# The first k by another queue in an attention and MLP kernel: fp32 load ahead of f, a split cast, the clamp on GpSimd

## The chip, the core and the metric

One core of one Trainium2 chip runs the kernel. The metric is the device time of one execution in microseconds; three timed runs gave 321.07, 321.27 and 321.29 us, median 321.27.

## What is computed

Eight batches of eight heads of attention with a forget gate (576 tokens, 64 columns a head), and behind it an MLP with GELU on the 4608 x 512 result:

```python
scores = scale * np.matmul(q, k.transpose(0, 1, 3, 2))
log_f = np.log(np.clip(f, 0.0001, 1.0))
cum = np.cumsum(log_f, axis=-1)
decay = cum[:, :, :, None] - cum[:, :, None, :]
scores = np.where(causal, -1000000000.0, scores + decay)
attn = softmax(scores)
x = np.matmul(attn, v)                 # heads side by side: 4608 x 512
out = gelu_tanh(x @ w_in) @ w_out      # 512 -> 2048 -> 512
```

q, k, v are fp32 (8, 8, 576, 64), f is fp32 (8, 8, 576), the weights are fp32, and the output is fp32 (4608, 512).

## The kernel before, in words

**Units.** Four heads are a quad, i = 0 to 15, two quads a batch. The MLP works on chunks c of 512 of the 4608 rows. Each batch's attention fills its part of `xT`, and the MLP takes its chunks from there. Matmuls are in bf16, the sums in PSUM in fp32.

**Order.** Everything is in an order written out by hand: `setup()` (line 703) issues the first instructions, and then `run` (line 844) reads tables of words, FRONT (line 71) for the first two quads, the first chunk and the way into the steady state, then SECOND, STEADY, FLUSH and LAST. Each word calls one entry of `ops` (line 786), which issues that step's instructions on whichever engines they run on. Each engine works through its own instructions in this order and waits on semaphores where it needs another's result. So the place of a word sets the place of its instructions in the queue of every engine it uses, the DMA queues of SyncE (SP) and GpSimd (POOL) among them.

**The words that matter here.**

- `B.n.cols` and `BK.i.n` (lines 255 and 261): n dummy matmuls into `idle_ps`, of 128, 256 or 512 columns; BK reads `kT`, so it waits for that transpose.
- `LP.t`: tile t (128 tokens) of v of batch 0 into `v_nat`; `LC` and `LV` are loads of v of later batches. `WI.c`, `WO.c`: pieces of the weights. `LK.i`, `LQ.i`: k and q of quad i. LP, LC, WI, WO, LK and LQ are on GpSimd's queue, and k, q and the weights are cast from fp32 to bf16 by the DMA.
- `TK.i`, `TQ.i` (lines 223 and 226): VectorE transposes `k_c` into `kT` and `q_c` into `qT`, in 32 x 32 blocks of 4-byte words.
- `SC` (line 727): the running sum of log f, a scan on VectorE. `CT` (line 745): TensorE transposes the sums into `cum_ps`. `CE.n` (line 751): ScalarE's exp of them, `wT`, for the first two quads (0) and the others (1). `w.0` and `W.0`: their bf16 copy `w_bf` on ScalarE or VectorE.
- `S.i.r` and `H.i.r.g` (line 267): scores of quad i, round r, for all heads or two of them (`ps_s`), with their exp on ScalarE into `pt`. `M` and `m`: the causal mask, on GpSimd or VectorE. For the first two quads the work is in four rounds of columns.
- `D.i.part` (line 364): the denominators, a product with `w_bf`, then transpose (`den`), reciprocal and transpose back on VectorE. `vw.i.part` (line 229): v times `wT` on VectorE. `V.i.x.part` (line 382): the product with `vw` and its scaling into `xT` on VectorE.
- `j`, `J`, `I`, `i`: the MLP's first product in parts, `F.c.n` and `f.c.n` its second, n steps; `f` splits each step's 128 columns of weights into four matmuls of 32.

**The start.** `setup()` issues f on SyncE's queue, then k of quad 0, q of quad 0, k and q of quad 1 on GpSimd's (`load_one`, line 207). VectorE fills constants, then clamps f (line 724), ScalarE takes its logarithm (line 725), and the first words go on from there: VectorE's order at the start is clamp, SC, TK.0, TQ.0, TK.1, TQ.1. TensorE's is 14 dummies, CT, dummies around TK.0 and TQ.0, and then S.0.0.

Of the kernel before, what the change touches and what calls it, by code (L numbers as in the profile page):

```python
# [16 lines left out]
def kernel(  # L17
# [69 lines left out]

    SECOND = """
        Y F.-1.99 T.0.1 T.0.2 LB.2.0 T.0.3 T.0.4 LB.2.1 I.0.0 LB.2.2 E.0.2.2 I.0.1 LB.2.3 TK.3 LK.5 LB.2.4 E.0.2.2 TQ.3 LQ.5 TQ.4 I.0.2 E.0.2.2 I.0.3
        E.0.2.1 TK.4 G.0 VW.3 I.0.6 I.0.7 G.1.1.2 X F.0.13 S.3.0 M.3.0 f.0.9 UW.0.1 D.2 f.0.9 S.3.1 M.3.1 V.2.0 f.0.12 S.3.2 M.3.2 CL.3 V.2.1 VW.4  # L90
        f.0.14 S.4.0 UW.0.2 M.4.0 D.3 f.0.10 V.3.0 UW.0.4 CL.4 UW.0.3 S.4.1 f.0.13 M.4.1 V.3.1 S.4.2 F.0.9 M.4.2 F.0.2 F.0.1
    """

    STEADY = """
        LK.4 LQ.4 Q.0.2 Y LB.2.0 T.0.1 T.0.2 LB.2.1 F.-1.2 Q.0.2 i.0.2.4 T.0.4 LB.2.2 i.0.2.4 T.0.3 Q.0.2 TQ.3 LQ.5 Q.0.2 F.-1.6 i.0.3.4 Q.0.2 Q.0.2
        LB.2.3 TK.3 LB.2.4 LK.5 i.0.3.4 Q.0.2 TK.4 TQ.4 F.-1.99 I.0.6 i.0.7 G.0 S.3.0 X G.1.1.2 f.0.16 M.3.0 D.2 VW.3 f.0.12 S.3.1 M.3.1 V.2.0 f.0.13
        S.3.2 M.3.2 CL.3 V.2.1 VW.4 f.0.15 S.4.0 D.3 f.0.10 V.3.0 M.4.0 CL.4 S.4.1 f.0.14 M.4.1 V.3.1 S.4.2 F.0.12 M.4.2
    """

    FLUSH = """  # L100
# [21 lines left out]
    def many(n, shape, dtype, name):  # L122
        return [singles.tile(shape, dtype, name=f"{name}{i}") for i in range(n)]
# [11 lines left out]
    vw = many(2, [128, NT + 1, 4, D], BF16, "vw")  # L135
# [4 lines left out]
    gT = singles.tile([128, N_FT, CH], BF16, name="gT")  # L140
# [7 lines left out]
    f_sb = f_all[0:BH, :]  # L148
# [58 lines left out]
    def load_one(src, dst, i):  # L207
        b, h0 = i // QPB, 4 * (i % QPB)
        return nc.gpsimd.dma_start(  # L209
            out=dst[i % 2].rearrange("p a d -> p (a d)"),  # L210
            in_=src[b, h0:h0 + 4].rearrange("h (p a) d -> (h p) (a d)", p=32))

    def transpose_words(src, dst):

        n = src.shape[1]
        return nc.vector.transpose(  # L216
            out=dst.rearrange("p s c -> p (s c)").bitcast(FP32)
                .rearrange("p (t a) -> p a t", a=n),
            in_=src.rearrange("p a d -> p (a d)").bitcast(FP32)
                .rearrange("p (a d) -> p a d", d=D // 2),  # L220
        )
# [15 lines left out]
    def copy_low(i, copy):  # L237
        return copy(vw[i % 2][64:128, LOW], vw[i % 2][0:64, 0])
# [462 lines left out]


    def setup():
        nc.sync.dma_start(out=f_sb, in_=f.rearrange("b h s -> (b h) s"))
        nc.scalar.preload_act_table_set("natural_log_exp_and_others")
        load_one(k, k_c, 0)
        load_one(q, q_c, 0)
        make_identity(nc, ident_f32)
        load_one(k, k_c, 1)
        load_one(q, q_c, 1)  # L710

        nc.vector.memset(idle, 0.0)
        nc.vector.memset(ones_f32, 1.0)
        nc.vector.memset(shift, -64.0)
        nc.vector.memset(wT[64:128, :, HIGH, :], 0.0)
        for t_ in kT:
            nc.vector.memset(t_[:, 0:64], 0.0)
            nc.vector.memset(t_[:, 64 + S:], 0.0)
        zeros()
        logs()  # L720
        idle_ps.append(psO.tile([128, 1024], FP32, name="idle_ps", tag="po"))

    def logs():
        nc.vector.tensor_scalar(f_sb, f_sb, 1e-4, 1.0, op0=ALU.max, op1=ALU.min)
        nc.scalar.activation(f_sb, f_sb, AF.Ln)

    def running_sums():
# [55 lines left out]
    def load_values(b, half):  # L783
# [112 lines left out]
```

## Time and profile before

The profiled execution's own numbers:

| | |
|---|---|
| time of the profiled execution | 321.58 us |
| span, first to last instruction | 319.9 us |
| granted TensorE clock, mean | 1.000 |
| PE, DVE, ACT, POOL busy | 314.1, 243.3, 213.0, 108.2 us |
| bytes moved by DMA | 33.41 MB in 47,491 packets |
| GpSimd's DMA queue (software) | 15.99 MB, 28.3% of 16 engines' span |
| SyncE's DMA queue (hardware) | 16.60 MB, 19.4% of 16 engines' span |

PE is TensorE's matmuls, DVE is VectorE, ACT ScalarE, POOL GpSimd, SP SyncE. In a row of the timeline stand the start and the duration in us from the span's start, engine, line, operation, output and inputs, shapes, and in brackets the idle time ahead of it with what ended it. A chain row has start, duration, engine, output and line, with the number of instructions merged. A row of transfers has the KB of one and the time from its issue to its landing.

### The profile page before, as it was taken

What the parts mean: (1) busy time and instruction counts of PE and PEld (TensorE: products, weight loads), DVE (VectorE), ACT (ScalarE), POOL (GpSimd) and SP (SyncE); (2) the same over time, 40 slices, a digit from 0 to 9 for tenths busy, and PEclk for the clock granted to TensorE, in tenths of its full rate; (3) what the DMA queues carried; (4) which work ended last, traced back from release to release, by engine and by line L of the source; (5) the groups of instructions that cost most, each with busy time, mean ns of one, the idle gap of its engine ahead of it and who ended that gap; (6) DMA issues with size and microseconds to landing.
All of it is one profiled execution on the core that took longest, in us unless ns stands there. A gap on an engine that the chain in (4) does not pass through costs nothing.

```text
span 319.9 us, 11741 instructions
## 1 busy us (share of the span) xinstructions
PE 314.1 (98%) x5292; PEld 220.7 (69%) x5311; DVE 243.3 (76%) x368; ACT 213.0 (67%) x248; POOL 108.2 (34%) x146
## 2 busy tenths in 40 slices
PE   8999999999999999999999999999999999999996
PEld 3467834445776567776778877767776786688785
DVE  7675638698978879879877998599886866597674
ACT  3676777866766776878667867787596744836610
POOL 8789625600340416400851065305610150000000
PEclk9999999999999999999999999999999999999999
DMA  7999998951273911594129411971002111010213
GB/s 125 229 199 196 207 234 202 220 150 37 54 130 103 200 22 37 115 209 77 37 75 223 104 39 30 209 160 38 5 33 68 35 33 38 24 43 2 98 35 99
DMA packets 47491, 33.41 MB, mean 104 GB/s; under 512 B 29777, under 2 KB 42193, under 8 KB 47441
## 3 DMA queue, kind: packets, MB, share of 16 engines
q0 software_dynamic: 9632, 15.99, 28.3%
q1 hardware_dynamic: 37664, 16.60, 19.4%
q8 instruction: 41, 0.67, 0.9%
q10 hardware_dynamic: 144, 0.07, 0.1%
q14 instruction: 10, 0.07, 0.1%
HBM read 36.85 MB, written 9.44 MB: 145 GB/s over the span
## 4 chain that ended last, share of the span: by engine, by line
PE 98%; DVE 1%; issue 1%
PE ps_w L619 31%; PE ps_h L403 19%; PE ps_s L285 10%; PE ps_q L539 10%; PE po L355 9%; PE ps_h L439 5%; PE pso L692 4%; PE ps_u L487 4%; PE idle_ps L258 3%; PE po_m L341 2%; PE ps_p L619 1%; PE ps_o L355 0%; PE idle_ps L264 0%; DVE xT L387 0%; PE cum_ps L749 0%
## 5 line engine op out<-in xcount | busy, mean ns | idle before, releaser
L293 ACT ACTIVATE pt<-ps_s 128x1024 bf16<-128x1024 f32 (+2 forms) x100 | 94.0, 991 | 37.5 <-PE ps_s L285 35.9
L299 POOL TENSOR_SCALAR_AFFINE_SELECT pt<-pt 128x512 bf16<-128x512 bf16 (+3 forms) x70 | 43.3, 629 | 108.3 <-ACT pt L293 85.6
L403 PE MATMUL ps_h<-xT,w_in_sb 128*128 128x512 bf16 (+1 forms) x307 | 65.5, 357 | 0.8 <-issue 0.2
L403 PEld LDWEIGHTS <-w_in_sb 128*128 128x128 bf16 x320 | 31.1, 98 | 26.5 <-issue 0.6
L411 ACT ACTIVATE gT<-ps_h 128x1024 bf16<-128x1024 f32 x34 | 34.6, 1018 | 20.3 <-PE ps_h L403 20.1
L619 PEld LDWEIGHTS <-gT 128*32 128x32 bf16 (+1 forms) x1177 | 43.9, 97 | 5.7 <-issue 2.2
L619 PE MATMUL ps_w<-w_out_sb,gT 128*32 128x256 bf16 (+1 forms) x996 | 42.7, 273 | 0.0
L619 PEld LDWEIGHTS <-gsum 128*32 128x32 bf16 (+1 forms) x909 | 35.1, 97 | 3.9 <-issue 1.7
L285 PE MATMUL ps_s<-qT,kT 32*128 32x64 bf16 (+5 forms) x896 | 35.2, 261 | 0.0
L555 DVE TENSOR_TENSOR usnap<-ps_q,usnap 128x1024 f32<-128x1024 f32 x15 | 17.9, 1221 | 17.3 <-PE ps_q L539 12.7
L619 PE MATMUL ps_w<-usum,gsum 128*32 128x256 bf16 (+1 forms) x752 | 29.8, 273 | 0.0
L233 POOL TENSOR_TENSOR vw<-v_nat,wT 128x1280 bf16<-128x1280 f32 (+1 forms) x12 | 27.4, 2279 | 2.7 <-DMA v_nat<-in_v_dram 2.4
L285 PEld LDWEIGHTS <-kT 32*128 32x128 bf16 x896 | 16.2, 92 | 16.8 <-issue 10.2
L636 DVE COPY snap<-ps_w 128x512 f32<-128x512 f32 x32 | 21.8, 682 | 6.5 <-PE ps_w L619 6.3
L550 ACT ACTIVATE gT<-usnap 128x1024 bf16<-128x1024 f32 x15 | 15.8, 1052 | 11.0 <-DVE usnap L555 10.7
L387 DVE TENSOR_TENSOR xT<-po,rb 128x576 bf16<-128x576 f32 x26 | 19.5, 751 | 4.6 <-PE po L355 4.4
L355 PE MATMUL po<-pt,vw 128*32 128x64 bf16 (+4 forms) x624 | 22.6, 278 | 0.0
L355 PEld LDWEIGHTS <-vw 128*32 128x32 bf16 x672 | 14.6, 97 | 9.6 <-issue 3.0
L216 DVE STREAM_TRANSPOSE kT<-k_c 128x576 f32<-128x576 f32 x16 | 19.4, 1244 | 2.1 <-DMA k_c<-in_k_dram 2.1
L216 DVE STREAM_TRANSPOSE qT<-q_c 128x576 f32<-128x576 f32 x16 | 19.8, 1245 | 0.3 <-DMA q_c<-in_q_dram 0.3
L209 POOL DMA_DIRECT2D k_c<-in_k_dram x16 | 9.1, 572 | 29.0 <-DVE kT L216 17.4
L539 PEld LDWEIGHTS <-w_in_sb 128*128 128x128 bf16 x160 | 15.6, 98 | 2.1
(135 smaller groups left out, 489.6 us busy)
## 6 DMA issues: line engine op xcount, KB each, us to landing
out_dram<-o_st SPq DMA_DIRECT2D x35, 256.0 KB, 2.2
k_c<-in_k_dram POOLq DMA_DIRECT2D x16, 288.0 KB, 5.5
q_c<-in_q_dram POOLq DMA_DIRECT2D x16, 288.0 KB, 6.6
v_nat<-in_v_dram SPq DMA_DIRECT2D x16, 256.0 KB, 5.3
v_nat<-in_v_dram SPq DMA_DIRECT2D x20, 128.0 KB, 5.3
v_nat<-in_v_dram POOLq DMA_DIRECT2D x8, 256.0 KB, 10.0
w_in_sb<-in_moe_w_in_dram POOLq DMA_DIRECT2D x8, 256.0 KB, 8.6
w_out_sb<-in_moe_w_out_dram POOLq DMA_DIRECT2D x4, 512.0 KB, 10.6
```

What stands on the lines that cost most here:

```text
L216: return nc.vector.transpose(out=dst.rearrange("p s c -> p (s c)").bitcast(FP32) .rearrange("p (t a) -> p a t", a=n), in_=src.rearrange("p ...
L233: return eng.tensor_mul(vw[i % 2][:, t0:t1], vb[:, t0:t1, h0:h0 + 4, :], wT[:, i, t0:t1, :].unsqueeze(3).to_broadcast([128, t1 - t0, 4, D]))
L285: nc.tensor.matmul(tiles[h // 2][:, h % 2, c0:c0 + nq], key_columns(i, key, h, c), qq[32 * h:32 * h + 32, q0:q0 + nq, c], start=(c == 0 an ...
L293: nc.scalar.activation(p[:, 2 * g:2 * g + 2, off:off + n], t[:, :, 0:n], AF.Exp, scale=scale)
L299: nc.gpsimd.affine_select(out=x, in_=x, compare_op=ALU.is_ge, fill=0.0, base=0, pattern=pattern, channel_multiplier=-1)
L355: nc.tensor.matmul(po[r0:r0 + w.shape[-1], 448 + q0:448 + q0 + nq], w, p[:, h, col:col + nq], start=(key in (0, "low")), stop=(key in ("lo ...
L387: nc.vector.tensor_mul(xT[:, 2 * u + x, r0 + s0:r0 + s1], po, rbs[i, part])
L403: nc.tensor.matmul(ph[:, j, n * cols:(n + 1) * cols], w_in_sb[:, dt, 128 * ft:128 * ft + 128], xT[:, dt, h0:h0 + cols], start=(dt == 0 and ...
L411: nc.scalar.activation(gelus(c, 2 * pr, 2), ph, AF.Gelu_apprx_tanh)
L539: nc.tensor.matmul(ps[:, k, HC * n:HC * n + HC], w[:, d, 128 * n:128 * n + 128], x[:, d, :], start=(first and n == 0 and d == 0), stop=(d ...
L619: nc.tensor.matmul(ps[c0:c0 + width, n, cols[0]:cols[1]], x[:, j, 128 * n + c0:128 * n + c0 + width], w[:, j, cols[0]:cols[1]], start=(fir ...
L636: copy(kept[name], ps)
```

## The change

k of quad 0 is loaded as fp32 by SyncE's queue, ahead of f, into memory that the GELU's output `gT` uses later; GpSimd's queue then begins with q of quad 0. The cast to bf16 is done by ScalarE (the right half of the columns) and by VectorE (the left half, as a product with ones), at the end of `setup()`. The clamp of f goes from VectorE to GpSimd, and clamp and logarithm become words of their own (`LG`, `LN`). FRONT is written anew in another order. The words of SECOND and STEADY are the same; only their lines are broken elsewhere. Lines behind the new code move down by up to 16.

```diff
+    first = gT.rearrange("p f n -> p (f n)").bitcast(FP32)[:, 0:S * D // 32]
+
+    def load_first():
+        nc.sync.dma_start(out=first, in_=k[0, 0:4].rearrange("h (p a) d -> (h p) (a d)", p=32))
+
+    def cast_first():
+        to, n = k_c[0].rearrange("p a d -> p (a d)"), 576
+        nc.scalar.copy(to[:, n:], first[:, n:])
+        nc.vector.tensor_mul(to[:, 0:n], first[:, 0:n], ones_f32[:, 0:1].to_broadcast([128, n]))
...
     def setup():
+        load_first()
         nc.sync.dma_start(out=f_sb, in_=f.rearrange("b h s -> (b h) s"))
         nc.scalar.preload_act_table_set("natural_log_exp_and_others")
-        load_one(k, k_c, 0)
         load_one(q, q_c, 0)
...
-        logs()
+        cast_first()
         idle_ps.append(psO.tile([128, 1024], FP32, name="idle_ps", tag="po"))
 
+    def clamp():
+        nc.gpsimd.tensor_scalar(f_sb, f_sb, 1e-4, 1.0, op0=ALU.max, op1=ALU.min)
+
     def logs():
-        nc.vector.tensor_scalar(f_sb, f_sb, 1e-4, 1.0, op0=ALU.max, op1=ALU.min)
         nc.scalar.activation(f_sb, f_sb, AF.Ln)
...
+        "LG": clamp,
+        "LN": logs,
```

The first words of FRONT, up to the first denominators, before:

```
B.1.128 B.1.512 B.1.256 SC B.8.512 B.1.256 B.1.512 B.1.128 LP.0 LP.1 CT B.2.512 WI.1 B.1.256 TK.0 B.1.128 B.1.128 BK.0.2 WI.0 LP.4
BK.0.1 B.1.512 CE.0 TQ.0 B.1.512 CE.1 LP.3 B.1.512 BK.0.1 S.0.0 B.1.128 B.1.128 LP.2 TK.1 M.0.0 w.0 WI.5 BK.0.1 B.3.512 WI.2 H.0.2.1
WI.3 B.1.128 TQ.1 BK.0.1 B.1.128 B.1.128 B.1.256 B.1.128 BK.1.1 B.1.512 H.0.1.0 WI.4 D.0.0 vw.0.0 vw.1.0 H.0.2.0 B.2.512 BK.1.1
```

and after:

```
LP.3 TK.0 B.1.128 B.1.512 LP.0 B.1.256 B.8.512 B.1.512 B.1.128 B.2.512 B.1.256 TQ.0 LG B.1.128 LP.1 LN SC TK.1 BK.0.2 S.0.0 B.1.512
BK.0.1 TQ.1 WI.1 B.1.512 BK.0.1 B.1.128 B.1.128 LP.2 H.0.2.0 BK.0.1 CT CE.0 W.0 WI.0 H.0.2.1 H.0.1.0 WI.3 WI.2 B.3.512 H.1.0.1 CE.1
B.1.128 B.1.128 B.1.128 B.1.128 vw.0.0 B.1.256 B.2.512 B.1.128 M.0.0 D.0.0 WI.4 H.1.0.0 LP.4 WI.5 M.1.0 LQ.2 H.0.1.1 M.0.1 WI.7
```

Further on, the same scores, masks, values and MLP parts stand in another order. In the output product of the first chunk (`pso`, line 692) 16 of its 64 steps are `F` and 48 `f`, where 31 and 33 were.

More of the change, by code (lines that the diff above doesn't have):

```diff
@@ new lines @@
+        V.0.0.0 V.0.1.0 BK.1.1 UT vw.1.0 B.1.128 B.1.512 H.0.3.0 B.1.512 H.0.3.1 D.1.0 H.1.2.0 M.0.3 V.1.0.0 WI.6 V.1.1.0 H.1.3.0 LK.2
+        j.0.0.4 H.1.1.0 H.1.3.1 j.0.0.4 j.0.0.8 RJ.0.0 M.1.3 H.1.2.1 VW.1.1 tr H.1.1.1 M.1.1 D.0.1 j.0.1.8 J.0.2 vw.0.1 GJ.0.0 j.0.1.8
+        V.0.0.1 LQ.3 V.0.1.1 PW.2.1 D.1.1 J.0.3 V.1.0.1 V.1.1.1 J.1.3 J.1.1 W.1 J.1.2 WO.0 F.0.1 WO.1 LK.3 GJ.0.1 WO.2 J.1.0 F.0.1 f.0.1
+        WO.3 TQ.2 LQ.4 TQ.3 U.0 f.0.1 LC.1.4 LC.1.1 f.0.1 LC.1.0 f.0.1 LC.1.3 f.0.1 LC.1.2 f.0.1 TK.2 LK.4 S.2.0 TK.3 f.0.10 S.2.2 M.2.2
@@ new lines @@
+        f.0.1 LK.5 f.0.8 S.2.1 PW.2.2 F.0.9 m.2.1 LV.2.1 S.3.0 m.2.0 vw.2 f.0.2 cl.2 LV.2.0 f.0.2 D.2 f.0.1 F.0.2 S.3.1 TK.4 f.0.4 LV.3.0
+        f.0.1 V.2.0 M.3.0 TQ.4 f.0.1 S.3.2 m.3.1 TK.5 VW.3 cl.3 LQ.5 F.0.1 LQ.6 F.0.1 M.3.2 f.0.3 V.2.1 UW.2.4 LK.6 f.0.1 S.4.1 f.0.6
+        H.4.2.0 D.3 VW.4 f.0.1 H.4.0.0 H.4.0.1 V.3.1 v.3.0 f.0.1 vw.5 H.4.2.1 F.0.1 I.1.0 U.1 U.2 I.1.4 TQ.5 I.1.5 LV.3.1 cl.4 U.3 I.1.1
+        I.1.3 F.1.2 TQ.6 G.0 I.1.6 I.1.2 I.1.7 TK.6 F.1.4 X G.1.1.2 F.1.7 S.5.0 LQ.7@m.3.1 F.1.2 M.4.2.3 LK.8 F.1.5 LK.7 F.1.2 m.4.2.2 F.1.5
@@ L98 @@
+        Q.0.2 Q.0.2 LB.2.3 TK.3 LB.2.4 LK.5 i.0.3.4 Q.0.2 TK.4 TQ.4 F.-1.99 I.0.6 i.0.7 G.0 S.3.0 X G.1.1.2 f.0.16 M.3.0 D.2 VW.3 f.0.12
+        S.3.1 M.3.1 V.2.0 f.0.13 S.3.2 M.3.2 CL.3 V.2.1 VW.4 f.0.15 S.4.0 D.3 f.0.10 V.3.0 M.4.0 CL.4 S.4.1 f.0.14 M.4.1 V.3.1 S.4.2 F.0.12
+        M.4.2
     """
```

28 lines of the change are left out of this document (8 added, 20 removed).

## The prediction

> **What bounds the kernel now.** I read the page first, then the chain of work that ended last.
>
> ```profile
> span 319.9 us, 11741 instructions
> ...
> PE 314.1 (98%) x5292; PEld 220.7 (69%) x5311; DVE 243.3 (76%) x368; ACT 213.0 (67%) x248; POOL 108.2 (34%) x146
> ...
> PE 98%; DVE 1%; issue 1%
> ```
>
> TensorE is busy, and on the chain, for 98% of the span. An edit elsewhere counts only if it lets TensorE start its real work earlier, or makes it wait. The profiled execution took 321.58 us, 1.7 us more than its span of 319.9; the three timed runs have a median of 321.27. I work out a difference and apply it to 321.27. The next view asks whether TensorE waits after the start: busy time by stretch.
>
> ```profile
> 16.00:30.00 14.00, 13.88 (x268) 9.41 (x264) 8.01 (x17) 11.52 (x16) 12.27 (x20) 1.00 1.17 196
> 30.00:45.00 15.00, 14.89 (x169) 10.28 (x167) 9.22 (x11) 9.92 (x10) 8.39 (x11) 1.00 1.18 221
> 45.00:60.00 15.00, 14.68 (x284) 6.56 (x277) 9.30 (x14) 11.42 (x15) 7.97 (x11) 1.00 0.99 210
> 60.00:75.00 15.00, 14.86 (x169) 7.13 (x164) 14.18 (x19) 10.79 (x13) 2.92 (x2) 1.00 0.69 157
> ```
>
> The first pair of numbers after the stretch is its length and TensorE's busy time. From 16 to 75 us TensorE idles 0.12 + 0.11 + 0.32 + 0.14 = 0.69 us in all. The last three columns are granted clock, DMA share and GB/s: the clock is full and the DMA engines are full until 60 us. So the reordered words have at most 0.7 us to win there; what can be won is in the first 16 us, where TensorE's busy time is partly dummies. The chain at the start, merged:
>
> ```profile
> 1.26 5.08 PE idle_ps L258 x14
> ...
> 6.38 0.69 PE cum_ps L749 x5
> 7.07 0.76 PE idle_ps L258 x5
> 7.83 0.65 PE idle_ps L264 x3
> 8.48 0.65 PE idle_ps L258 x3
> 9.12 0.22 PE idle_ps L264
> 9.34 0.45 PE ps_s L285 x16
> ...
> 10.88 0.39 PE ps_s L285 x4
> ...
> 12.35 0.56 PE ps_s L285 x8
> 12.91 0.28 PE po_m L341 x8
> ```
>
> `idle_ps` is a dummy. The first real product, S.0.0, starts at 9.34 (call it S), behind dummies; 0.69 us of real work (CT, `cum_ps`) stands ahead of it. What releases S is on the other engines:
>
> ```profile
> 0.81 0.58 SPq L704 DMA_DIRECT2D f_all<-in_f_dram  x1
> ...
> 1.30 0.72 POOL L209 DMA_DIRECT2D k_c<-in_k_dram  x1 [0.79 <-POOLq L880]
> ...
> 3.68 0.45 DVE L724 TENSOR_SCALAR f_all<-f_all 64x576 f32<-64x576 f32 x1 [0.19 <-DMA f_all<-in_f_dram]
> 4.17 0.68 ACT L725 ACTIVATE f_all<-f_all 64x576 f32<-64x576 f32 x1 [2.08 <-DVE f_all L724]
> 4.25 1.81 POOL L186 DMA_DIRECT2D v_nat<-in_v_dram  x2
> ...
> 4.88 1.35 DVE L728 TENSOR_TENSOR_SCAN f_all<-ones_f,f_all 64x576 f32<-64x576 f32 x1 [0.75 <-ACT f_all L725]
> 6.16 1.22 DVE L216 STREAM_TRANSPOSE kT<-k_c 128x576 f32<-128x576 f32 x1
> 7.24 1.22 DVE L216 STREAM_TRANSPOSE qT<-q_c 128x576 f32<-128x576 f32 x1
> ...
> 13.24 0.45 DVE L374 STREAM_TRANSPOSE den<-po_m 128x256 f32<-128x256 f32 x1 [0.85 <-PE po_m L341]
> ...
> 14.33 1.25 DVE L233 TENSOR_TENSOR vw<-v_nat,wT 128x512 bf16<-128x512 f32 x2
> ```
>
> VectorE runs clamp, scan, TK.0, TQ.0, and TQ.0 ends at 7.24 + 1.22 = 8.46. TensorE could begin then; its own dummies hold it 0.88 us longer. The transfers, with the time from issue to landing:
>
> ```profile
> f_all<-in_f_dram SPq DMA_DIRECT2D x1, 144.0 KB, 2.9
> ...
> k_c<-in_k_dram POOLq DMA_DIRECT2D x1, 288.0 KB, 4.1
> q_c<-in_q_dram POOLq DMA_DIRECT2D x1, 288.0 KB, 5.0
> ```
>
> f lands at 0.81 + 2.9 = 3.7. The first k is issued at 1.30 and lands at 5.4; VectorE, in its scan until 6.2, isn't waiting for it. q is issued next and lands at 7.0.
>
> **The sum.** With one TensorE order before and one after, the change in time is: later or earlier S, plus real work that moves behind S, plus dummies added behind S, plus new waits.
>
> *CT* moves behind S: +0.69 (row above). *Dummies*: the front words before hold 11,008 columns of dummies ahead of S.0.0 and 7,680 behind; the words after hold 8,064 and 7,936. Behind S that is 256 more, at 0.65/3 us per 512 columns (row at 8.48): +0.11. So the change pays only if S comes before 9.34 - 0.69 - 0.11 = 8.54.
>
> *S after.* VectorE now does the cast's half, TK.0, TQ.0. Let T be the landing of the fp32 k. The cast's VectorE half is 576 fp32 columns to bf16; the nearest row is vw at 14.33, two of 512 columns in 1.25, so 0.63 x 576/512 = 0.70. ScalarE's half is nearest to its own 576-column row, 0.68, and lies beside it. TK.0 and TQ.0 took 8.46 - 6.16 = 2.30. With 0.1 us for each of the waits on the DMA, on the casts and on TQ.0, S = T + 0.70 + 2.30 + 0.3 = T + 3.3. q, now first on GpSimd's queue, must be there by T + 2.0; it moves up one issue (0.72 us), to about 6.3, and is in time. TensorE's own floor: 7,040 columns of leading dummies at the slow starting rate (5.08 us for 5,888 columns) end at 1.26 + 6.07 = 7.33, and two more dummies after TK.0 make 7.76.
>
> *T* is the unknown: 576 KB by SyncE's queue, four times f. No row shows such a load, so from both sides. The view of the first 3.9 us of DMA, in slices of about 0.1 us:
>
> ```profile
> GB/s 0 1 0 0 0 0 0 0 0 0 0 0 0 0 0 0 0 0 0 0 0 0 165 142 165 71 331 355 284 213 71 24 24 95 142 118 189 142 118 260
> ```
>
> f's bytes begin at 2.2, are through by 3.0 at up to 355 GB/s, and the landing at 3.7 is 0.7 later. k alone at 355 GB/s: 590 KB take 1.66, so 2.2 + 1.66 + 0.7 = 4.5. That is the near end. The far end is sharing: GpSimd's queue delivers its first bytes at about 2.7, now q's, on the same 16 engines. A stretch of 0.5 us from 110 us, where both queues have work:
>
> ```profile
> q0 software_dynamic: 43, 0.09, 100.7%
> q1 hardware_dynamic: 36, 0.01, 10.4%
> ```
>
> q0 is GpSimd's queue, q1 SyncE's: 43 packets against 36, so they take turns by packet. The Trainium skill ("DMA: Bandwidth & Descriptors", Queues, rings and completion order) says that each DMA engine goes round the rows that have work, a packet at a time; the trace agrees (43 to 36), and it speaks against "ahead of f, ahead of everything". If q halves k's rate from 2.7 on, the 0.5 us before have moved 0.5/1.66 of k, the rest takes 2 x 1.16, and T = 2.7 + 2.32 + 0.7 = 5.7. I take T = 4.95, nearer to the end alone, because GpSimd's queue starts slowly: between 3.0 and 3.8 the slices show 24 to 189 GB/s with nothing else running. Then S = 8.25 and the gain is 8.54 - 8.25 = **0.3 us**. (The skill's same page, section Anatomy of one DMA, fits 2.0 us plus bytes over 436 GB/s; an estimate from it has k landing at 4.2 and the gain at TensorE's floor. Its 2.3 us for f is not what the row shows, 2.9.)
>
> *f behind k.* f's landing goes to about T + 0.8 = 5.8. The clamp on GpSimd: no such row; below is VectorE's 0.45, above GpSimd's two-input 768-column product:
>
> ```profile
> 24.60 1.52 POOL L233 TENSOR_TENSOR vw<-v_nat,wT 128x768 bf16<-128x768 f32 x1
> ```
>
> 1.52 x 576/768 = 1.14. I take 0.9, as it has one input. Then Ln, 0.68: done at 7.6. The scan now stands behind TQ.0, at 8.2, so this is covered by 0.6 us; and CT, the next to want it, stands behind S.0.0, 1.0 us of dummies and H.0.2.0, at about S + 2, while scan ends at 9.6. Cost nothing; if the clamp took 1.5 us longer, CT would be late by about 0.5. Taking the clamp from VectorE gains nothing either: it is ahead of the wait for k.
>
> *GpSimd's queue.* The clamp waits for f and holds back the issue of LP.1 and every load after it. It costs nothing while the engines have earlier loads to move: at 6.7 us k1, q1, LP.3, LP.0 are still ahead. W.0 on VectorE instead of ScalarE (0.2 us) is covered by the same dummies.
>
> *F to f.* 15 steps of the output product change from one 128-column matmul to four of 32. By form:
>
> ```profile
> L692 PE MATMUL pso<-w_out_sb,gT 128*32 128x512 bf16 x132 | 9.3, 381 | 0.0
> L692 PE MATMUL pso<-w_out_sb,gT 128*128 128x512 bf16 x27 | 7.2, 380 | 0.4 <-issue 0.3
> ```
>
> 9.3/33 = 0.28 against 7.2/27 = 0.27 a step: +0.2 at most, and as much may come back from fewer changes between the two shapes. I take 0. The remaining words are the same products in another order, with 0.69 us of idle time to win or to double.
>
> Sum: 8.25 - 9.34 + 0.69 + 0.11 = -0.29; 321.27 - 0.3 = **321.0 us**.
>
> **The rivals.**
>
> *k has the engines to itself.* T = 4.5, S = 7.8, at TensorE's floor: 7.8 - 8.54 = -0.74, and up to half of the 0.69 us idle with it: 320.2 to 320.6. For it: q's slow start. Against it: the packets in turn.
>
> *A new wait takes over: VectorE's vw.0.0.* It now stands ahead of the denominators' transpose (den), and needs LP.0 and LP.1. LP.1, the second of the two `v_nat` issues at 4.25, used to be issued at 5.2; now it stands behind the clamp, at 6.7 or later. The loads' rows:
>
> ```profile
> v_nat<-in_v_dram POOLq DMA_DIRECT2D x1, 256.0 KB, 7.8
> ```
>
> If that time from issue holds, LP.1 lands at 14.5, vw.0.0 ends at 15.2, and den, which TensorE would release at S + 5.7 (2.9 of products by the rows above, 6,272 columns of dummies 2.7, 0.1 of waits) + 0.3 = 14.2, starts 1.0 late; with f at 6.4, 1.6 late. That gives +0.7 to +1.3: 322.0 to 322.6. It decides if LP.1 lands after 13.5. Against it: LP.1 is the sixth load of the queue as before, when it landed at 5.2 + 7.8 = 13.0, so the time is set by what is ahead, not by its issue.
>
> *The change doesn't do what it says.* Sharing in full, T = 5.7, later than the software queue's 5.4: S = 9.0, +0.45: 321.4 to 321.8.
>
> **How the numbers follow.** Chances: the forecast 0.42 (its own range 320.7 to 321.4), k alone 0.28, the wait of vw.0.0 0.19, full sharing 0.11. About 0.2%, 0.64 us, is what a measurement of this kernel can tell from no change: faster lies below 320.63, slower above 321.91. The forecast gives 0.06 faster, 0.34 same, 0.02 slower; k alone 0.26 and 0.02; the wait is slower; full sharing 0.08 same, 0.03 slower. Together 0.32, 0.44, 0.24. The range, 319.9 to 322.3, leaves out the best of the reordering together with k alone, and the worst of the wait.
>
> **What would show it.** The landing of gT's load (4.5, 4.95 or 5.7); the first `ps_s` at T + 3.3; idle time of PE ahead of it where before there were dummies; `vw` ahead of `den` with a wait for a DMA or none; the scan with no wait ahead of it. I am wrong if S lies under 7.7, if TensorE's idle time from 16 to 75 us leaves 0.3 to 1.4, or if the scan waits for Ln.

## The result, and the profile after

The changed kernel takes 323.60 us (median of nine runs, 321.23 to 323.97) against 321.27 for the kernel before on the same chip: a ratio of 1.0055, 95% interval 1.0032 to 1.0078. It is slower, and the time lies above the forecast's range. (The ratio goes by the means, 322.94 and 321.17 us, and so lies below that of the medians; in e2 and e3 below it leaves out one disturbed run each, of 362.52 and 326.77 us.) The profiled execution took 323.97 us, 2.4 more than that of before: 1.8 in the span and 0.6 around it. Its page, with the lines shown of before:

```profile
span 321.7 us, 11794 instructions
PE 313.2 (97%) x5317; PEld 220.8 (69%) x5336; DVE 243.8 (76%) x367; ACT 214.0 (67%) x249; POOL 112.2 (35%) x147
PE 84%; DMA 9%; POOL 2%; ACT 2%; issue 1%; DVE 1%; DVEq 0%; POOLq 0%
```

The span is 1.8 us longer and TensorE is 0.9 us less busy. The chain, 98% TensorE before, now also runs over transfers and GpSimd. Busy time by stretch (columns as in the prediction):

```profile
16.00:30.00 14.00, 13.84 (x233) 9.12 (x233) 8.43 (x17) 12.61 (x19) 13.23 (x21) 1.00 1.11 178
30.00:45.00 15.00, 14.77 (x231) 10.84 (x226) 9.08 (x14) 8.82 (x10) 8.69 (x12) 1.00 1.12 179
45.00:60.00 15.00, 14.39 (x286) 6.62 (x283) 9.01 (x13) 10.84 (x13) 7.86 (x9) 1.00 1.02 225
60.00:75.00 15.00, 14.78 (x201) 7.20 (x199) 13.80 (x15) 11.60 (x13) 4.64 (x6) 1.00 0.91 197
```

From 16 to 75 us TensorE idles 0.16 + 0.23 + 0.61 + 0.22 = 1.22 us, against 0.69. This measure is rough: a second profile of the kernel before (e18 below) shows 0.14 us there, and it has records of 5311 matmuls where the first has 5292; a matmul without a record can count as idle time. The rest of the loss lies earlier, in the timeline of the start:

```profile
0.80 0.39 SPq L218 DMA_DIRECT2D gT<-in_k_dram  x1
...
1.30 0.74 POOL L211 DMA_DIRECT2D q_c<-in_q_dram  x1 [0.79 <-POOLq L896]
...
4.81 0.67 ACT L222 CAST k_c<-gT 128x576 bf16<-128x576 f32 x1 [2.73 <-DMA gT<-in_k_dram]
4.89 0.76 DVE L223 TENSOR_TENSOR k_c<-gT,ones_f 128x576 bf16<-128x576 f32 x1 [1.37 <-DMA gT<-in_k_dram]
...
5.76 1.26 DVE L228 STREAM_TRANSPOSE kT<-k_c 128x576 f32<-128x576 f32 x1
...
7.07 0.59 PE L276 MATMUL idle_ps<-kT,idle 128*128 128x512 bf16 x2 [0.57 <-DVE kT L228]
...
7.22 2.14 POOL L736 TENSOR_SCALAR f_all<-f_all 64x576 f32<-64x576 f32 x1 [1.84 <-DMA f_all<-in_f_dram]
...
8.07 1.26 DVE L228 STREAM_TRANSPOSE qT<-q_c 128x576 f32<-128x576 f32 x1 [1.06 <-DMA q_c<-in_q_dram]
9.39 0.83 PE L297 MATMUL ps_s<-qT,kT 32*128 32x256 bf16 x16 [1.73 <-DVE qT L228]
...
9.39 0.68 ACT L739 ACTIVATE f_all<-f_all 64x576 f32<-64x576 f32 x1 [3.91 <-POOL f_all L736]
9.42 0.94 POOL L188 DMA_DIRECT2D v_nat<-in_v_dram  x1
10.11 1.35 DVE L742 TENSOR_TENSOR_SCAN f_all<-ones_f,f_all 64x576 f32<-64x576 f32 x1 [0.78 <-ACT f_all L739]
...
14.27 1.00 DVE L245 TENSOR_TENSOR vw<-v_nat,wT 128x512 bf16<-128x512 f32 x1
...
16.58 0.45 DVE L386 STREAM_TRANSPOSE den<-po_m 128x256 f32<-128x256 f32 x1 [1.31 <-PE po_m L353]
```

The fp32 k lands at 4.8 and its cast and transpose are done at 7.0. Then VectorE waits 1.06 us for q, which the forecast had in place at 6.3 and which lands at 8.05. TensorE, out of dummies, waits 1.73 us and starts S.0.0 at 9.39, where the kernel before has it at 9.27. f lands at 7.14, the clamp on GpSimd takes 2.14 us, and the load behind it (LP.1) is issued at 9.42. The scan, at 10.11, waits for the logarithm.

The two waits of TensorE have a second price. The granted clock, third column from the right:

```profile
8.00:10.00 2.00, 0.61 (x16) 0.41 (x15) 1.26 (x1) 0.61 (x1) 1.94 (x2) 0.74 1.08 215
10.00:12.00 2.00, 2.00 (x14) 0.73 (x6) 1.89 (x2) 1.59 (x3) 2.00 (x4) 0.50 1.02 269
12.00:14.00 2.00, 2.00 (x25) 0.99 (x22) 1.72 (x3) 1.20 (x4) 2.00 (x3) 0.91 1.08 198
```

After 0.57 + 1.73 us of waiting the clock is halved for about 3.4 us ((0.26 + 0.50 + 0.09) x 2 us / 0.50). The Trainium skill ("TensorE: Matmul & The Clock Gate", Part 1: The HAM clock gate) says that the activity is judged in a free-running window of some 3.4 us. The traces agree in so far as the length of the waits alone doesn't decide: of the runs below, e7 waited 1.99 us in one piece and its clock fell, e9 waited 1.49 us and e4 even 2.76 + 0.49 us, and both kept theirs.

Where the 1.9 us come from can be added up, because TensorE's last matmul ends at S, the start of S.0.0, plus all that TensorE does and waits for behind it. (S is 9.27 before by the timeline; the prediction's 9.34 is the chain's figure for the same matmul.) Summed over TensorE's rows, in us, the second and third profiles being further executions of the same kernel:

| | S | waits behind S | dummies behind S | CT behind S | other products | end |
|---|---|---|---|---|---|---|
| before | 9.27 | 1.52 | 3.58 | 0 | 302.55 | 316.92 |
| before, second profile (e18) | 9.93 | 0.14 | 3.68 | 0 | 303.55 | 317.30 |
| after | 9.39 | 2.12 | 4.63 | 0.44 | 302.25 | 318.83 |
| after, second profile (e5) | 8.33 | 3.10 | 3.68 | 0.49 | 302.48 | 318.08 |
| after, third profile (e12) | 9.18 | 1.99 | 4.64 | 0.44 | 302.22 | 318.47 |

Between the first profiles, S gives +0.12 where the forecast had -1.09; waits +0.60; dummies +1.05, of which about 0.1 are the added columns and the rest is the halved clock; CT +0.44; other products -0.30. In the second profile of the changed kernel q came at 7.00, S at 8.33, close to the forecast's 8.25, and the clock stayed full. Even so the end is 1.2 us later than before: waits and other products together are 1.5 us longer. (They are better taken together, since a matmul without a record moves time from the one to the other, as the two profiles of before show.)

A mark that does not depend on missing records is the first product of the steady state, the first `ps_u`. From there to its last matmul TensorE takes 215.07 to 215.38 us in every profile of this document. From S to there it takes 92.6 and 92.3 us in the two profiles of before, and 94.4, 94.7 and 94.2 in the three after: 1.7 to 2.4 us more, where the forecast had 0.80. So two things have to be explained: q's arrival, and what takes longer between S and some 104 us.

### The profile page after: what moved, and what is told of

Read it like the earlier page. It is cut to its first block, busy times and chain, and to the rows that moved or that the text cites. A ratio compares the mean times of both kernels' runs of the same rounds, so it can differ in the third digit from the quotient of the medians.

```text
span 321.7 us, 11794 instructions
## 1 busy us (share of the span) xinstructions
PE 313.2 (97%) x5317; PEld 220.8 (69%) x5336; DVE 243.8 (76%) x367; ACT 214.0 (67%) x249; POOL 112.2 (35%) x147
## 4 chain that ended last, share of the span: by engine, by line
PE 84%; DMA 9%; POOL 2%; ACT 2%; issue 1%; DVE 1%; DVEq 0%; POOLq 0%
PE ps_w L631 31%; PE ps_h L415 19%; PE ps_q L551 10%; PE po L367 9%; PE ps_s L297 8%; PE ps_u L499 4%; DMA v_nat<-in_v_dram 4%; DMA k_c<-in_k_dram 3%; DMA q_c<-in_q_dram 2%; ACT pt L305 1%; PE idle_ps L270 1%; PE pso L704 1%; PE ps_p L631 1%; PE ps_o L367 0%; POOL w_out_sb L204 0%
## 5 line engine op out<-in xcount | busy, mean ns | idle before, releaser
L305 ACT ACTIVATE pt<-ps_s 128x1024 bf16<-128x1024 f32 (+2 forms) x100 | 94.1, 990 | 34.8 <-PE ps_s L297 34.7
L311 POOL TENSOR_SCALAR_AFFINE_SELECT pt<-pt 128x512 bf16<-128x512 bf16 (+3 forms) x71 | 45.8, 654 | 89.6 <-ACT pt L305 66.7
L297 PE MATMUL ps_s<-qT,kT 32*128 32x64 bf16 (+5 forms) x896 | 36.1, 263 | 1.9 <-DVE qT L228 1.7
L211 POOL DMA_DIRECT2D k_c<-in_k_dram x15 | 8.4, 558 | 32.9 <-DVE kT L228 31.0
```

Source lines behind the costliest of these rows:

```text
L297: nc.tensor.matmul(tiles[h // 2][:, h % 2, c0:c0 + nq], key_columns(i, key, h, c), qq[32 * h:32 * h + 32, q0:q0 + nq, c], start=(c == 0 an ...
L305: nc.scalar.activation(p[:, 2 * g:2 * g + 2, off:off + n], t[:, :, 0:n], AF.Exp, scale=scale)
L311: nc.gpsimd.affine_select(out=x, in_=x, compare_op=ALU.is_ge, fill=0.0, base=0, pattern=pattern, channel_multiplier=-1)
```

## The experiments

My theory after reading this profile: the load of k on SyncE's queue holds q back on GpSimd's, S is not earlier for it, and TensorE cools while it waits. The rivals: the clamp on GpSimd and the loads behind it set the end; or the new order of the words does. Each kernel is timed beside the kernel before on the same chip (medians 321.05 to 321.11).

**The words without the load (e1).** k goes back to GpSimd's queue, no cast; clamp on GpSimd and all new words stay.

```diff
     def setup():
-        load_first()
...
+        load_one(k, k_c, 0)
         load_one(q, q_c, 0)
...
-        cast_first()
```

> The changed kernel, but k of quad 0 comes by GpSimd's software queue in bf16 again, ahead of q, and there is no cast. The new words and the clamp on GpSimd stay. Theory A (the software queue's first load stands still while the hardware queue moves k and f, so q lands at 8.05, S.0.0 isn't earlier, and TensorE cools down while it waits): the software queue's first packet is back near 2.7 us, k lands near 5.4, q near 7.0, S.0.0 starts near 8.6, and the time is 321.0 to 322.2. Rival B (the new word order costs the time by itself): 322.8 or more. Rival C (the clamp on GpSimd holds the loads back): f lands at 3.7, so the clamp runs at about 6.1 to 8.2 and LP.1 is issued 1.2 us earlier than in the changed kernel; about 322.5.

Measured: 322.02 us, ratio 1.0029 (1.0018 to 1.0040). q lands at 7.42, S is at 8.76. The time is within what the theory allowed, but the words with the clamp are slower than before by themselves, and without the load q comes earlier, not later, than in the profile after.

**Dummies against the cold clock (e2).**

```diff
-... LN SC TK.1 BK.0.2 S.0.0 B.1.512
+... LN SC TK.1 BK.0.9 S.0.0 B.1.512
```

> The changed kernel with seven more dummies (BK.0.9 for BK.0.2) in TensorE's wait between TK.0 and S.0.0. Theory A: S.0.0 stays at 9.4, the granted clock stays 1.00 between 8 and 12 us, D.0.0 comes at about 15.0 instead of 16.2, and the time falls by 0.8 to 1.5 us, to 322 to 322.8. B and C: the half clock is covered by other waits, and the time stays within 0.4 us of the changed kernel's.

Measured: 324.69 us, ratio 1.0104 (1.0088 to 1.0120), above all three medians of the changed kernel (323.60, and 322.73 and 323.02 in e5 and e12 below). The clock was full throughout, but q landed at 8.60, so S was at 9.93, and TensorE then waited 0.25 us for the scan and 0.40 for the mask. Another 1.2 us went behind the last matmul (4.1 us to the end of the span against 2.9; the last `o_st` transfers to DRAM took 3.7 us from issue to landing against 2.2), which the edit doesn't touch. From S to the first `ps_u` this execution takes 94.1 us against 94.4 after. So a full clock won little here: where the cold clock stretched dummies in the profile after, TensorE waits here, for the scan and the mask. The last part of my theory isn't borne out, though q's late landing clouds the comparison.

**The clamp on VectorE (e3), and f ahead of k (e4).**

```diff
     def clamp():                                # e3
-        nc.gpsimd.tensor_scalar(f_sb, f_sb, 1e-4, 1.0, ...)
+        nc.vector.tensor_scalar(f_sb, f_sb, 1e-4, 1.0, ...)
     def setup():                                # e4
-        load_first()
         nc.sync.dma_start(out=f_sb, ...)
+        load_first()
```

> The changed kernel with the clamp on VectorE, at its new place behind TQ.0. Theory A: the clamp waits for TQ.0 at 9.3, scan is 0.4 us later, LP.1 and the loads behind it are issued 4 us earlier (5.4), but S.0.0 stays at 9.4 and the clock still falls: within 0.5 us of the changed kernel. Rival C: the loads' gain is the point, the weights land 1 us or more earlier, and the time falls by 0.8 us or more.

> The changed kernel with f ahead of k on SyncE's queue. Theory A: f lands at 3.7, k at about 5.2, the software queue's first packet is still held back until about 4.2, q lands at 8.0 to 8.2, S.0.0 at 9.4 to 9.6; time within 0.5 us of the changed kernel. Rival C: the clamp no longer waits for f, it ends near 7.6 instead of 9.4, LP.1 is issued 1.8 us earlier, and the time falls by 0.7 us or more. If the queues only took turns, q would land near 7.

Measured: e3 322.25 us, ratio 1.0036 (1.0025 to 1.0047); e4 323.76, ratio 1.0071 (1.0049 to 1.0094). With the clamp off GpSimd, LP.1 is issued at 5.3 instead of 9.4, and the time is 0.5 to 1.3 us below the changed kernel's three medians, or 0.5 to 0.8 by the ratios, which lies between the theory (within 0.5) and the rival (0.8 or more). LP.1 itself lands no sooner for it (13.78 against 14.18 after and 13.34 in e5). In e4 f lands at 3.84 but k only at 6.50, so S is at 9.86, and q lands at 7.01. That misses the theory, which wanted k at 5.2 and q at 8.0 to 8.2; it is what taking turns was said to give. GpSimd's first packet comes at 3.91, with less than half of k moved, and then both queues move packets, here from 4.4 to 5.2 us (q0 is GpSimd's queue, q1 SyncE's):

```profile
q0 software_dynamic: 36, 0.08, 55.4%
q1 hardware_dynamic: 37, 0.16, 51.0%
```

**The changed kernel again (e5, e12).** No edit; two more profiles on two more occasions.

> The changed kernel once more, as the measure for the runs beside it. Both theories: 322.9 to 324.0 us, first real product at 9.4, q landing at 8.0, granted clock near 0.5 from 10 to 12 us. If in a second profile the clock stays full there and the time does not fall, the cold clock is not part of the loss.

> The changed kernel a third time, as the measure for the runs beside it and for how far its own start varies: 322.5 to 323.7 us, runs 1.5 us or more apart; f landing between 5.5 and 7.6 and q between 7.0 and 8.6, S.0.0 at q's landing plus 1.3.

Measured: 322.73 us, ratio 1.0061 (1.0037 to 1.0084), and 323.02, ratio 1.0051 (1.0032 to 1.0069). q landed at 7.00 and at 7.84, f at 6.19 and 7.15; e5 missed the expected 8.0 for q and 9.4 for S. The granted clock of each timed run is on record too. Of the 22 runs of the changed kernel in its three timings, six show 0.989 to 0.995, with a mean of 323.9 us, and sixteen show 0.999 or 1.000, with a mean of 322.6; no run of e1, and none of the kernel before in all these timings, shows less than 0.998. The fallen clock and the late q come together in the profiles (8.05 and 7.84 against 7.00), so this doesn't separate them. Together they add 0.4 us to the mean of 322.9, and without such runs the changed kernel is still 1.4 us slower than before.

In e5 nothing is cold and S is early, so its timeline shows what else waits:

```profile
8.33 0.52 PE L297 MATMUL ps_s<-qT,kT 32*128 32x256 bf16 x16 [0.54 <-DVE qT L228]
...
11.52 1.23 DVE L228 STREAM_TRANSPOSE qT<-q_c 128x576 f32<-128x576 f32 x1
...
12.60 0.16 DVE L793 CAST w_bf<-wT 128x40 bf16<-128x40 f32 x1
...
12.80 0.51 PE L297 MATMUL ps_s<-qT,kT 32*128 32x256 bf16 x8 [0.26 <-DVE w_bf L793]
13.13 1.69 POOL L311 TENSOR_SCALAR_AFFINE_SELECT pt<-pt 128x512 bf16<-128x512 bf16 x2
...
13.44 0.90 DVE L245 TENSOR_TENSOR vw<-v_nat,wT 128x512 bf16<-128x512 f32 x1 [0.68 <-DMA v_nat<-in_v_dram]
...
14.87 0.23 PE L353 MATMUL po_m<-pt,w_bf 128*1 128x128 bf16 x4 [0.41 <-POOL pt L311]
```

The first of S.0.0's exps have been ready since 9.8, but GpSimd masks them only at 13.13: behind the clamp (to 8.42) stand 4.7 us of issuing held-back loads. TensorE waits 0.41 us for the mask, and 0.26 ahead of H.1.0.1. The profile puts these 0.26 us down to W.0 (`w_bf`), but H.1.0.1 reads `qT`, not `w_bf`, and TQ.1 ends at 12.75, just as long before it. TQ.1 stands on VectorE behind the scan, which waits for clamp and logarithm.

**The kernel before without four dummies (e6).**

```diff
-BK.0.1 B.1.512 CE.0 TQ.0 B.1.512 CE.1 LP.3 B.1.512 BK.0.1 S.0.0
+BK.0.1 CE.0 TQ.0 CE.1 LP.3 S.0.0
```

> The kernel before without the four 512-column dummies that stand between TK.0 and S.0.0 (one ahead of TQ.0, three behind it); nothing else changes. Theory A (the start of S.0.0 sets the end, TensorE then being busy throughout): S.0.0 starts when qT is ready, 8.5 instead of 9.3, and the time falls by 0.6 to 0.9 us: 320.3 to 320.6. Theory B (behind S.0.0 the products wait for other things, so that its start is worth little): the gap comes back ahead of the denominators or the first products of the MLP, and the time falls by under 0.3.

Measured: 320.61 us (320.46 to 321.08), ratio 0.9985 (0.9976 to 0.9993). It is faster than both kernels.

```profile
8.51 0.52 PE L285 MATMUL ps_s<-qT,kT 32*128 32x256 bf16 x16 [0.24 <-DVE qT L216]
```

S moves from 9.27 to 8.51 and the last matmul from 316.92 to 316.04. So TensorE's own dummies held S, and an earlier S is worth most of its amount: 0.76 us of S gave 0.9 between these profiles and 0.5 between the medians, which is between the two expectations. The change sought it in the wrong place.

**Half of k on each queue (e7).** SyncE loads two of the four heads, GpSimd's queue the other two ahead of q; the cast covers 64 partitions.

```diff
-        nc.sync.dma_start(out=first, in_=k[0, 0:4]...)
+        nc.sync.dma_start(out=first[0:64], in_=k[0, 0:2]...)
...
+        nc.gpsimd.dma_start(out=k_c[0].rearrange("p a d -> p (a d)")[64:128], in_=k[0, 2:4]...)
         load_one(q, q_c, 0)
```

> The changed kernel with only half of the first k (two of four heads) as fp32 by SyncE's queue; the other half is GpSimd's first load, cast by the DMA. Theory A (GpSimd's queue moves no bytes until SyncE's k is through): its first packet comes at 3.1 to 3.4 us, between 2.7 (k not there) and 4.06 (all of k); f lands at 4.9 to 6.3 and q at 7.4 to 7.8, S.0.0 starts at 8.6 to 9.0, and the time is 0.4 to 0.8 below the changed kernel's. Theory B (queues take turns from the start, and q is late for another reason, its place behind GpSimd's wait for instance): first packet at 2.7 or at 4.06 whatever the bytes, and q not earlier than 8.0.

Measured: 323.57 us, ratio 1.0064 (1.0046 to 1.0082). Packets by queue from 2.7 to 3.7 us, for before, after and e7:

```profile
q0 software_dynamic: 42, 0.10, 84.5%
q1 hardware_dynamic: 31, 0.04, 10.7%
```

```profile
DMA packets 89, 0.37 MB, mean 371 GB/s; under 512 B 6, under 2 KB 6, under 8 KB 89
...
q1 hardware_dynamic: 89, 0.37, 93.3%
```

```profile
q1 hardware_dynamic: 57, 0.18, 54.8%
q0 software_dynamic: 33, 0.08, 47.0%
```

GpSimd's queue (q0) moves nothing in this microsecond in the changed kernel. Its first packet comes at 2.73 us with f alone on SyncE's queue (144 KB), at 3.10 with half of k (288 KB), and at 4.06 (3.82 in e5) with all of k (576 KB): it starts when SyncE's k is nearly through. (In e4, where k comes behind f, it doesn't: 3.91, with more than half of k to come. So k's end isn't what starts it, and what is stays open.) The first theory's number holds for the start (3.1 to 3.4 expected). It misses for q, at 8.16 instead of 7.4 to 7.8, for S, at 9.50 instead of 8.6 to 9.0, and for the time.

**The weights' loads early (e8), and the mask early (e9).**

```diff
 # e8
-... V.1.1.0 H.1.3.0 LK.2
+... V.1.1.0 H.1.3.0 LK.2 WO.0 WO.1
 # e9
-... B.1.128 LP.2 H.0.2.0 BK.0.1 CT CE.0 W.0 WI.0 ... M.0.0 D.0.0
+... B.1.128 M.0.0 LP.2 H.0.2.0 BK.0.1 CT CE.0 w.0 WI.0 ... D.0.0
```

> The changed kernel with the words of the first two loads of the second product's weights (WO.0, WO.1) put back behind LK.2, where the kernel before has them. Theory A (the new words issue these loads 6.7 us later, the DMA engines run dry from 28 to 32 us, and TensorE waits for data between 38 and 60): GB/s from 28 to 32 us goes from 60 to 130 up to some 200, TensorE's idle time from 30 to 60 us falls from 0.84 to 0.4 to 0.6, and the time falls by 0.2 to 0.4 us. Theory B (that idle time comes from the order of products and scores, not from loads): idle time and time within 0.15 us of the changed kernel's.

> The changed kernel with the mask M.0.0 put ahead of four loads in GpSimd's order (behind LP.1 and WI.1, ahead of LP.2) and the copy w_bf back on ScalarE (w.0 for W.0). Theory A (behind S.0.0 TensorE waits for what the change has queued: the mask behind GpSimd's clamp and its loads, 0.41 us, and w_bf behind VectorE's transposes, 0.26 us): both waits are gone, the denominators start 5.2 to 5.5 us after S.0.0 instead of 5.8, and the time is 0.4 to 0.8 below that of the changed kernel beside it. Theory B (these waits only take the place of waits that come a little later): another wait of 0.4 to 0.7 appears by 21 us, time within 0.3 of the changed kernel's.

Measured: e8 322.94 us, ratio 1.0067 (1.0044 to 1.0091), beside 322.73 for e5; e9 324.04, ratio 1.0088 (1.0067 to 1.0109), beside 323.02 for e12. In e8 the loads behave as the first theory said (205 GB/s and more from 28 to 32 us, idle time from 30 to 60 us 0.62 instead of 0.84, 0.4 to 0.6 expected), but the median doesn't follow. In e9 the wait for the mask is gone from its place and others stand a little later, with the loads that the mask now holds back. The 0.26 us ahead of H.1.0.1 stay, with the copy on ScalarE, and the profile now names TQ.1:

```profile
13.68 0.52 PE L297 MATMUL ps_s<-qT,kT 32*128 32x256 bf16 x8 [0.26 <-DVE qT L228]
...
18.45 0.29 PE L353 MATMUL po_m<-pt,w_bf 128*32 128x256 bf16 x4 [0.21 <-POOL pt L311]
19.03 0.23 PE L353 MATMUL po_m<-pt,w_bf 128*1 128x128 bf16 x4 [0.29 <-POOL pt L311]
```

The second theory holds for the waits: shifting GpSimd's work about only moves them. For the time it doesn't, which is 1.0 us above e12's instead of within 0.3.

**All three mended (e10), and the same without the load (e11).** Clamp on VectorE, w.0, WO.0 and WO.1 early; e11 also has k on GpSimd's queue without the cast, as e1.

> The changed kernel with the clamp on VectorE, w.0 for W.0 and WO.0, WO.1 back behind LK.2: the fp32 load, the split cast and the other new words stay. Theory A (with these waits mended, only S.0.0 and the 0.80 us of work moved behind it count): S.0.0 at 8.3 to 8.8, no wait over 0.2 us from there to 30 us, and 320.7 to 321.6 us, level with the kernel before. Theory B (the fp32 load itself costs, by the spread that it brings into the arrival of f and q): 321.8 to 322.6 with a spread of over 1 us.

> As the mended kernel, but with the first k cast by GpSimd's queue again: no fp32 load, no casts. Beside the mended kernel this is the worth of the load alone. If q sets S.0.0 in both (Theory A), S.0.0 is at 8.6 to 8.8 here and at most 0.3 later or earlier there, and the times differ by under 0.3 us; here 320.9 to 321.6. If the load were worth what its T of 4.8 promised (S.0.0 at 8.25), this kernel would be 0.4 to 0.6 slower than the mended one. If the load costs (Theory B), it is 0.5 to 1.0 faster, and its runs lie closer together.

Measured: 323.09 us, ratio 1.0059 (1.0047 to 1.0071), and 322.94, ratio 1.0067 (1.0043 to 1.0090). Neither is the level that the first theory wanted. S is at 8.51 and 8.67, but both have a wait that no other kernel shows, here in e10 (0.94 us in e11):

```profile
48.49 0.40 PE L297 MATMUL ps_s<-qT,kT 32*128 32x64 bf16 x5 [1.00 <-issue]
```

What TensorE waits for there the profile doesn't show, and the product has records of only 16 of its 24 matmuls. These two can't be used for the start, except for one thing: they differ by the load alone, and the load gains nothing (323.09 with, 322.94 without).

**Start against rest (e13, e14, e15).** The words up to the first product of the MLP's output, at 39 us, from one kernel, and all behind them in the order of the other. e13 is the changed kernel with the old rest, e14 the same without the load and cast, e15 the kernel before with the new rest.

```diff
 # e13, e14: the changed kernel's first 110 words, and then
-J.1.2 WO.0 F.0.1 WO.1 LK.3 GJ.0.1 WO.2 J.1.0 F.0.1 f.0.1 ...
+J.1.2 WO.0 WO.1 GJ.0.1 TQ.2 J.1.0 U.0 WO.2 LK.3 WO.3 LC.1.0 PW.2.2 F.0.3 LC.1.3 f.0.2 ...
 # e15: the first 126 words of before, and then
-PW.2.1 PW.2.2 F.0.3 LC.1.3 f.0.2 ...
+PW.2.1 PW.2.2 F.0.1 F.0.1 f.0.1 LQ.4 TQ.3 f.0.1 ... TK.2 LK.4 S.2.0 ...
```

> The changed kernel up to the first product of the MLP's output (39 us), and from there the words of the kernel before, in their order. If the loss lies in the start (the load, the clamp on GpSimd, the first 110 words): 322.5 to 323.7, as the changed kernel. If it lies in the rest (F against f, the other order from 39 to 75 us): 321.2 to 322.0.

> The same, but with the first k by GpSimd's queue and cast there: the clamp on GpSimd and the first 110 words alone. Beside the words-only kernel (322.0), which differs by the rest alone. Loss in the start: 321.6 to 322.2. Loss in the rest: 320.9 to 321.4.

> The kernel before up to the first product of the MLP's output (39 us), and from there the words of the changed kernel: none of the load, the casts, the clamp. Loss in the start: 320.9 to 321.3, level with the kernel before. Loss in the rest: 321.6 to 322.3, and TensorE's idle time from 45 to 60 us about 0.5 us, as in the words-only kernel, against 0.32 before.

Measured: e13 322.67 us, ratio 1.0053 (1.0034 to 1.0073); e14 322.36, ratio 1.0035 (1.0022 to 1.0048); e15 328.50, ratio 1.0225 (1.0209 to 1.0241). The first two stay where the changed kernel and e1 are, so the loss lies in the start. e15 says nothing of the rest: at the seam TensorE waits for `kT`, whose transposes stand on VectorE behind TQ.3, and TQ.3 waits 5.83 us for its q.

```profile
45.16 1.15 PE L285 MATMUL ps_s<-qT,kT 32*128 32x64 bf16 x24 [4.41 <-DVE kT L216]
```

**The start taken apart (e16, e17, e18).** e16 is e13, and e17 is e14, with the clamp on VectorE (the edit of e3); so e17 has nothing of the change but its first 110 words (with the clamp as one of them). e18 is the kernel before.

> New start with the fp32 load, old rest, clamp on VectorE at its new place (behind TQ.0). If what is left is the clamp on GpSimd: 1.0 to 1.6 us below the new start with the clamp on GpSimd (322.67), so 321.1 to 321.7. If it is the load or the order of the first words: 322.0 or more. A wait of TensorE for the scan (CT) would show the clamp's price on VectorE, 0 to 0.3.

> The same without the load: the first 110 words in the new order, all else as in the kernel before (clamp on VectorE, k by GpSimd's queue, old words from 39 us on). The sum's own terms for them are S.0.0 at 8.5 to 8.8 instead of 9.3, 0.80 us of work moved behind it, so 0 to +0.3: 321.1 to 321.5. If the order itself costs more (waits behind S.0.0): 321.8 to 322.4. Its distance to the kernel with the load beside it is the load's own worth.

> The kernel before, for a second profile. Its runs lie within 0.8 us of each other, so S.0.0 should stand at 9.0 to 9.35 again and the span at 319.3 to 320.0: that is how far one profile of it may be taken as the measure.

Measured: e16 322.15 us, ratio 1.0026 (1.0011 to 1.0041); e17 322.15, ratio 1.0041 (1.0024 to 1.0059); e18 321.28, ratio 1.0002 (0.9994 to 1.0011). The first words alone cost 1.1 us, though their S is at 8.55. With the clamp on VectorE the load adds nothing to them by the medians (e16 against e17; the ratios are 1.0026 and 1.0041). With the clamp on GpSimd it adds 0.3 (e13 against e14; 1.0053 and 1.0035), and the changed kernel (1.0051 to 1.0061) lies 0.7 to 1.0 us above e1 (1.0029), which lacks the load. The clamp on GpSimd adds 0.2 without the load by the medians, nothing by the ratios (e14 against e17), and 0.5 by the medians, 0.9 by the ratios, with it (e13 against e16). That fits a price that load and clamp have only together, since the load brings f later and the clamp on GpSimd waits for f; but the intervals of each pair overlap, so it isn't shown. e18 missed its S:

```profile
9.93 0.52 PE L285 MATMUL ps_s<-qT,kT 32*128 32x256 bf16 x16 [0.97 <-DVE qT L216]
```

In that execution of the kernel before q landed at 8.60, and S at 9.93. Its time, 321.96 us, was the longest of its eleven runs. q's arrival varies from profile to profile: 6.90 to 8.60 in four profiles without the load and with the old words, 7.13 to 7.42 in four without the load and with the new, 7.00 to 8.60 in the twelve with all or half of the load. It is never at 6.3.

## Why the prediction was wrong

**The landing of k was right.** 4.79 us against T = 4.95, with 4.92 and 5.19 in the other two profiles. So were the casts (0.76 and 0.67 against 0.70 and 0.68), TK.0 and TQ.0 (2.4 in e5, where they follow each other, against 2.3), and, as far as the records go, the added dummies where the clock was full (3.68 - 3.58 = 0.10 against 0.11, but e18 has 3.68 too). CT measured 0.44 to 0.49 where I had 0.69. TensorE's floor was too high: the leading dummies ended at 6.50, not 7.33, so TensorE stood idle ahead of S for longer than the text had room for. The fit set beside T, of the Trainium skill ("DMA: Bandwidth & Descriptors", Anatomy of one DMA), is one for GpSimd's path; for SyncE's load it gave 4.2, which the trace doesn't bear out.

**The step that failed first is "q ... moves up one issue (0.72 us), to about 6.3, and is in time".** The formula S = T + 3.3 holds only while TQ.0 follows TK.0 at once. q landed at 8.05, S = 8.05 + 1.34. I had argued with packets in turn, from a row at 110 us, and asked only how far q would slow k. The runs showed the opposite: k slowed q. GpSimd's queue starts later, the more SyncE's is given first (first packet 2.73, 3.10 and 4.06 us for 144, 288 and 576 KB), and f and q then come together. The place gained in GpSimd's queue, 7.05 - 5.44 = 1.6 us by the landings before, was lost by a start 1.1 to 1.3 us later and a load that took longer (3.2 to 4.0 us from its first packet to its landing, against 2.7 for k before). The Trainium skill's rule of a packet at a time ("DMA: Bandwidth & Descriptors", Queues, rings and completion order) spoke against the change. The start of this trace doesn't show it at work, 89 packets to none, though e4 does a little later, 36 to 37; whether GpSimd's queue had anything ready at the start, no view shows.

**The second step that failed is the term for new waits behind S, which the sum put at nothing: "covered" for the clamp and "costs nothing" for GpSimd's held-back issues, and "the same products in another order" for the words.** The sum said 8.54 is the S that pays. e5 has 8.33 and e17 8.55, and both are slower than before. From S to the first `ps_u` they take 94.7 and 93.9 us against 92.6 and 92.3 before: 1.3 to 2.4 us more, where the sum had 0.80. I took 0.9 us for the clamp, with a bound of 1.14 from a two-input row with twice the partitions; it took 2.14. With f landing at 6.2 to 7.1 instead of 5.8, it is done at 8.4 to 9.4, GpSimd issues the held-back loads in one go, and the mask M.0.0, which the text did not name among what is queued behind the clamp, comes 3.3 us after its input. The scan, which was to start at 8.2 with 0.6 us to spare, starts at 9.2 to 10.1 and waits for the logarithm, and TQ.1 behind it comes 0.26 us late in e5. What did hold is that the loads themselves lose nothing: LP.1, issued at 9.42, landed at 14.18, and issued at 5.84 (e17) at 14.26. W.0 on VectorE delayed nobody that a row shows. I asked of each edit whether the next reader was late, but not what else stands in the same engine's queue.

**"F to f" at nothing** was not refuted (in the second chunk four steps went the other way, f to F): the kernels with the old rest (e13, e14) are 0.1 to 0.9 us below the changed kernel and 0.3 above e1, on both sides of nothing. Of the 0.5 us more of idle time from 16 to 75 us, e8 took away some 0.2 by issuing loads earlier, and was not faster; and two profiles of the kernel before differ by as much.

**The rivals.** "k alone" had T near right and failed with q. "Full sharing" named k as the one to suffer. "A new wait of vw.0.0" came nearest in time (322.0 to 322.6), and its condition was met (LP.1 landed at 14.18, later than 13.5). But it isn't what happened: in the profile after vw.0.0 is done at 15.27, and den starts at 16.58, released by TensorE. Of the three signs of being wrong, one came true in the profile after: the scan waits for Ln, 0.78 us. It was looked for as a cost to CT, and of the kernels with the new words CT waits for the scan only in e2 (0.25 us); the costs were elsewhere. The list lacked the other sign that came true, a wait for q ahead of TQ.0.

**What stays open.** Of the 1.1 us of the first words alone, the profile of e17 shows 0.6 at the last matmul (317.48 against 316.92), or 0.2 against the second profile of before. A profile is one execution of many that differ by q's arrival, and those of the kernel before lie at the long end of its own runs. In e15, which has the old start, S is 9.11; with that and e18's 92.3 us behind it the kernel before would end at 316.5, 1.0 us ahead of e17. That is an estimate, but it leaves little unplaced. Of e17's 1.3 to 1.6 us more behind S, CT and the added dummies are 0.6, the wait for TQ.1 0.26 and a wait for ScalarE's exp at 62.7 us 0.22; the rest is in pieces that no row names. How much of the changed kernel's further 0.6 to 1.4 us belongs to the load, to the clamp and to the cold clock isn't separated.

## What to carry to other kernels

Here, moving a load to another queue didn't make its partner arrive sooner: look for the last of the operands that the first product needs, and cost that one. Before a start is rebuilt, take away the dummies that hold it back; here four words less gave 0.5 us, and the rebuilt start lost 1.1. Take more than one profile of the kernel before: S stood at 9.27 in one and at 9.93 in the other. When an operation goes to an engine that also issues loads and makes masks, list all that stands behind it in that engine's queue, and time the operation by a row of that engine.

## What the runs showed of the hardware

- An fp32 load of 576 KB on SyncE's queue moved at about 371 GB/s from 2.7 to 3.7 us. GpSimd's queue, with its first load issued at 1.30, began to move packets at 4.06 instead of 2.73, and at 3.91 where that load stood second on SyncE's (e4); from then on both queues moved, 36 packets and 37 in 0.8 us.
- The clamp of 64 x 576 fp32 elements took 2.14 us on GpSimd and 0.45 on VectorE.
- The granted clock fell to 0.50 after waits of 0.57 and 1.73 us between 6.5 and 9.4 us, and was full again some 3.4 us later; it stayed full through waits of 2.76 and 0.49 us in e4. Keeping it full (e2) did not make the kernel faster.
- q's landing varies between executions of the same kernel: 7.05 and 8.60 us in two of the kernel before, 7.00 to 8.05 in three of the changed one.
